# Filler matmuls, new gates for the weight loads, row-sum trips on another queue, and group sums by TensorE, in a fused attention and feed-forward kernel

## The chip, the cores and the metric

The kernel runs on one core of a Trainium2 chip. The metric is the device time of one execution in microseconds; before the change it was measured in three runs. The core's engines are TensorE (PE in the profile), VectorE (DVE), ScalarE (ACT), GpSimd (POOL) and SyncE (SP). Each works through its own instructions in order, and they meet through semaphores. DMA transfers are issued by an engine's queue (here SP's and POOL's).

## The reference

```python
def sm_attn(qq, kk, vv):
    s = scale * np.matmul(qq, kk.transpose(0, 1, 3, 2))
    s = s - np.max(s, axis=-1, keepdims=True)
    a = np.exp(s)
    a = a / (np.sum(a, axis=-1, keepdims=True) + 1e-09)
    return np.matmul(a, vv)
q_d = q.reshape(B, H, Sd, factor, D).mean(axis=3)      # factor 4; k_d, v_d likewise
out_up = np.repeat(sm_attn(q_d, k_d, v_d), factor, axis=2)
mask = np.abs(pos[:, None] - pos[None, :]) < factor
...                                                    # masked softmax attention: out_local
attn_out = out_up + out_local
x = attn_out.transpose(0, 2, 1, 3).reshape(B * S, H * D)
h = x @ w_in
out = (h * (1.0 / (1.0 + np.exp(-h))) @ w_out).astype(np.float32)
```

The inputs q, k and v have the shape (8, 8, 576, 64), float32; w_in is (512, 2048), w_out (2048, 512), and the output (4608, 512).

## The kernel before

The 64 heads are worked in 32 pairs; four pairs make a batch of 576 tokens by 512 features, which is what the feed-forward part takes. For each pair, SP loads q and k (names `qk`), the value rows in four pieces (`vs`), and from pair 8 on the values once more in groups of four rows (`vq`, three issues). Pairs 1 to 3 come as bf16 straight from POOL's queue (`SW`). POOL casts to bf16 (`qkb`, `vb`). TensorE transposes (`pe_T`, L785 for the transposes), VectorE and ScalarE copy the results out of PSUM (`qT`, `kT`), and the sums over groups of four rows (`qd`, `kd`) are made in one of two ways: for pairs below `GS_PE` = 8 by TensorE inside `pe_T`, with a selection matrix `idp`, and copied out (`group`); for later ones by two VectorE reductions (`reduce`, L830). Then come scores (`pe_S`), exponentials on ScalarE (`Pt` local, `Pd` grouped), row sums (`pe_Z`), reciprocals on VectorE (`zr`, L947), and the weighted values (`pe_PV1`, `pe_PV2`).

The reciprocals must be spread over partitions. Pairs below 8 do it by TensorE (`RB`). Later ones make a trip through DRAM: `z{p}` writes `zr` to `scr`, then two DMAs `b{p}0` and `b{p}1` read it back, each half broadcast to 64 partitions of `Rb`; all three are issued by SP (`Z_ENG`), in `after_Z`. VectorE multiplies (`xo`, L999) and POOL adds the two parts into `xT` (L1026), the feed-forward input.

The feed-forward part has nine super-blocks of 512 tokens. `g1` is the hidden layer, 16 units of four 128x512 matmuls each, followed by tanh on ScalarE (`th`, L1052) and a product on VectorE (`gT`, L1056); `g2` is the output layer, 16 units again, then a copy (`osb`) and a store from SP. G1 of super-block 0 needs pairs 0 to 3, of 1 pairs 0 to 7, of 2 pairs 0 to 11. All of w_in and w_out come in eight chunks from POOL's queue (`weights`, `w0` to `w7`; `w0` to `w3` are w_in, 1 MB each); the first unit of G2 needs `w4` to `w7`.

The order on every engine is written by a planner before the program is built. A job has engines, a planned cost, jobs before it (`pre`), buffers and PSUM banks that it takes, and a due time; `Plan.run` steps through time, gives each engine the ready job with the least due time (on TensorE, `pick` chooses between attention work, `A` and `V` jobs, and G1 and G2 units), and the emitted instructions run in that order on the chip, with the semaphores that the data need. TensorE's planned costs are multiplied by `COLD[1]` before `COLD[0]` us. Planned DMA transfers share one flow. From pair 8 on a visit (`V{n}`) joins the scores of pair n, the transposes of n + 1, the row sums of n - 1 and the weighted values of n - 2, and comes when 8 (n - 10) units of G1 and G2 are done, or when nothing else can run.

Two settings gate loads. `W_GATE` says after which jobs a weight chunk may be issued: `w0` and `w1` after none, `w2` after the cast `cq5`, `w3` after `cq6`, the others after `cq7`. `load_order` gives the loads' order on SP and their gates: pair 1 waits for the cast `ck1`, pairs 4 to 7 for the issue of pair 3's last v piece, pairs 8 and 9 until chunk `w5` has landed, pairs 10 and 11 until `w6` has. A gate on a landed transfer is a semaphore wait on the issuing queue, and everything behind it in that queue waits too.

Of the kernel before, what the change touches and what calls it, by code (L numbers as in the profile page):

```python
# [19 lines left out]
COLD = (26.0, 1.5)  # L20
N_QK, N_VS, N_VQ, N_QKB, N_VB, N_VD, N_T, N_P, N_ZR, N_RB, N_XO = 3, 4, 2, 5, 5, 5, 3, 4, 2, 4, 2
GS_PE = 8
# [12 lines left out]
Z_ENG = "SP"  # L35
CV_ENG = ("POOL", "ACT")
# [4 lines left out]
def G2_BANKS(j):  # L41
    return ((5,), (4,), (2,), (3,)) if j >= 7 else ((4,), (5,))
# [44 lines left out]
W_GATE = {0: (), 1: (), 2: ("cq5",), 3: ("cq6",), **{c: ("cq7",) for c in range(4, 8)}}  # L87
# [6 lines left out]
def load_order():  # L94
    o = ["kx", ("qk", 0), ("qk", 1), ("qk", 2), ("qk", 3), ("v", 0), ("v", 1), ("v", 2), ("v", 3)]
    for p in range(4, NPAIR):
        o += [("qk", p), ("v", p)] + ([("vq", p)] if p >= VP_PE else [])
    return o, {1: ["ck1"], **{p: ["lv311!"] for p in range(4, 8)}, **{p: ["w6"] for p in range(10, 12)}, 8: ["w5"], 9: ["w5"]}
# [129 lines left out]
class Job:  # L228
    __slots__ = ("name", "eng", "cost", "emit", "pre", "take", "use", "due", "work", "port", "kind", "bank", "marks",
                 "idx", "n", "succ", "start", "end", "ran", "last", "thr")  # L230

    def __init__(self, name, eng, cost, emit, **kw):
# [4 lines left out]
        self.due, self.work, self.port, self.kind, self.thr = 0.0, 0.0, False, None, None  # L237
        for k, v in kw.items():
            setattr(self, k, v)
        self.ran, self.last, self.succ, self.end = None, None, [], None  # L240


class Plan:
# [5 lines left out]
    def __init__(self):  # L249
        self.jobs, self.pools, self.bind = {}, {}, {}  # L250
        self.banks = [None] * 8
        self.seq = []
# [56 lines left out]
    def run(self, pick):  # L309
# [37 lines left out]
        def release(k):  # L347
# [3 lines left out]
            if k[0] == "bank":  # L351
                for b in self.bind[k]:
                    self.banks[b] = None
# [15 lines left out]
        def flow(now):  # L369
            live = [q for q in queues.values() if q]  # L370
            dt, t = now - fluid[0], fluid[0]
            while live and dt > 1e-9:
                step = min(min(q[0][1] for q in live) * len(live), dt)
                for q in live:
                    q[0][1] -= step / len(live)
# [10 lines left out]
            if live:  # L386
                v = fluid[1]
                at(now + min(q[0][1] for q in live) * len(live) + 1e-6, lambda v=v: v == fluid[1] and flow(clock[0]))
# [8 lines left out]
        def dispatch(e, now):  # L397
# [12 lines left out]
            for x in j.eng:  # L410
                ready[x].remove(j)
            self.grab(j)
# [45 lines left out]
def bass_hourglass_attn__then__act_silu_kernel(  # L458
# [9 lines left out]
    with kctx:  # L468
# [21 lines left out]
        osb = sb("osb", [128, 512], F32, 2)  # L490

# [155 lines left out]
        def dma(name, eng, out_, in_, r, w, sem, work, cost, hold=(), **kw):  # L647
            def emit(j):
                P.op(eng, lambda s: s.dma_start(out_(), in_()), r() if r else [], w(), sem(), after=gates(hold))  # L649
# [3 lines left out]
        def loads(p, order):  # L653
            if p == 0:
                dma("lkx", "SP", lambda: kx[64:128, :], lambda: rows(k, 0, 64, 0), None, lambda: rkx, lambda: "kx",
                    0.45, 0.43, due=order["kx"], take=[("qkb", -1)])
            for x, (t, n, off) in enumerate(((q, 128, 0), (k, 128 if p < NPAIR - 1 else 64, 64))):
                if p in SW:
                    dma(f"c{'qk'[x]}{p}", "POOL", lambda x=x, n=n: qkb[S("qkb", p)][0:n, x, :],
                        lambda t=t, n=n, off=off: rows(t, p, n, off), None, lambda x=x: [R(f"qkb{S('qkb', p)}{x}")],  # L660
                        lambda x=x: f"qkb{S('qkb', p)}{x}", 0.9, 0.9, take=[("qkb", p)], due=-60 + p)
                    continue
                dma(f"l{'qk'[x]}{p}", "SP", lambda x=x, n=n: qk[S("qk", p)][0:n, x, :],
# [3 lines left out]
            for h in range(2):  # L667
                for j in range(2):
                    def emit(jb, h=h, j=j):
# [5 lines left out]
                        if (p, h, j) == (0, 0, 0):  # L675
                            lo = 1
                            P.op("SP", lambda e: e.dma_start(vs[s][3:64, 0, :], bass.AP(
                                tensor=T_, offset=base.offset, ap=[[64, 61], [1, 64]])), [], w, sem, after=gates(["vz"] + list(order.get(("gate", p), ()))))
                        if (p, h, j) == (NPAIR - 1, 1, 1):
                            hi = 4  # L680
                            P.op("SP", lambda e: e.dma_start(vs[s][64:123, 9, :], bass.AP(
                                tensor=T_, offset=base.offset + 517 * D_, ap=[[64, 59], [1, 64]])), [], w, sem)
                        P.op("SP", lambda e: e.dma_start(d[:, lo:hi, :], bass.AP(  # L683
                            tensor=T_, offset=o + 58 * 64 * lo, ap=[[64, 64], [58 * 64, hi - lo], [1, 64]])), [], w, sem,
                            after=gates(order.get(("gate", p), ())))
                    J(f"lv{p}{h}{j}", "SP", 0.61, emit, work=0.39, take=[("vs", p)],
                      due=order["v", p], pre=list(order.get(("gate", p), ())) + (["vz"] if p == 0 else []))
            if p >= VP_PE:
# [10 lines left out]
                J(f"lvq{p}", "SP", 1.4, emit, work=1.0, take=[("vq", p)], due=order["vq", p],  # L699
                  pre=list(order.get(("gate", p), ())) + [f"vqz{(p - VP_PE) % N_VQ}"])  # L700

        def weights(c, due, pre):
# [10 lines left out]
            J(f"w{c}", "POOL", 0.9, emit, work=3.2, due=due, pre=pre)  # L713
# [230 lines left out]
        def after_Z(p, key, i, col_):  # L944
# [9 lines left out]
            J(f"r{p}", "DVE", 1.15 if p < RB_PE else 0.6, emit, pre=[f"Z{p}"] + (["ga", "gb"] if p < RB_PE else []),  # L954
              bank=[(key, ())], take=[("zr", p)], due=D(p, 4.0))
            if p < RB_PE:
                return
            dma(f"z{p}", Z_ENG, lambda: scr[S("Rb", p)][:, :], lambda: zr[S("zr", p)][:, :],
                lambda: [R(f"zr{S('zr', p)}")], lambda: [R(f"scr{S('Rb', p)}")], lambda: f"scr{S('Rb', p)}", 0.25, 0.43,
                pre=[f"r{p}"], use=[("zr", p)], take=[("Rb", p)], due=-1000 + p, kind="hot")  # L960
            for h in range(2):
                dma(f"b{p}{h}", Z_ENG, lambda h=h: Rb[S("Rb", p)][half(h), :],
                    lambda h=h: bass.AP(tensor=scr[S("Rb", p)].tensor, offset=scr[S("Rb", p)].offset + 64 * h * 72,
                                        ap=[[0, 64], [1, 720]]),
                    lambda: [R(f"scr{S('Rb', p)}")], lambda h=h: [R(f"Rb{S('Rb', p)}{h}")],
                    lambda h=h: f"Rb{S('Rb', p)}{h}", 0.6, 0.43, pre=[f"z{p}"], use=[("Rb", p)], due=-1000 + p, kind="hot")
# [10 lines left out]
        def RB(p, wants):  # L977
# [3 lines left out]
            def emite(jb):  # L981
# [3 lines left out]
                     [R(f"Rb{n}0"), R(f"Rb{n}1")])  # L985
            J(f"RB{p}", "PE", 0.4, emit, pre=[f"r{p}", "rsel2"], use=[("zr", p)], bank=[(("r", p), wants)], due=D(p, 2.8), kind="A")
            J(f"b{p}0", ("ACT", "DVE"), {"ACT": 0.8, "DVE": 0.85}, emite, pre=[f"RB{p}"], bank=[(("r", p), ())], take=[("Rb", p)],
              due=D(p, 2.4), marks={f"b{p}1": 1.0})
# [4 lines left out]
        def after_PV(p):  # L993
# [3 lines left out]
            def emitm(jb):  # L997
# [3 lines left out]
                    [rB[bb[0]], rB[bb[1]], R(f"Rb{u}0"), R(f"Rb{u}1")], [R(f"xo{x}")])  # L1001
# [26 lines left out]
            J(f"m{p}", "DVE", 0.92, emitm, pre=[f"PV{p}", f"b{p}0", f"b{p}1"], bank=[(("o", p), ())], use=[("Rb", p)],  # L1028
# [9 lines left out]
        def g1(j, f):  # L1038
# [24 lines left out]
            J(f"t{j}_{f}", "ACT", 0.61, emitt, pre=[f"g1_{j}_{f}"], bank=[(key, ())], take=[("th", n)], due=-2000 + n)  # L1063
            J(f"s{j}_{f}", "DVE", 0.70, emits, bank=[(key, ())], use=[("th", n)], due=-2000 + n,
# [222 lines left out]
```

## Time and profile before

| what | value |
|---|---|
| median of three runs | 406.34 us (404.93, 406.34, 406.6) |
| the profiled execution | 403.24 us, span 401.4 us |
| TensorE busy | 346.7 us (86% of the span) |
| VectorE, ScalarE, GpSimd busy | 226.2, 170.2, 155.0 us |
| mean granted clock of TensorE | 0.960 |
| G1 matmuls (576) | 176.6 us, 435 ns each |
| G2 matmuls (576) | 143.1 us, 387 ns each |

The span runs from the first to the last instruction. Matmuls overlap in the pipeline, so the mean of one is longer than its share of the time. "SPq" is SP's queue: time in which it issues a DMA or waits to. "issue" is time in which an engine waited for nothing that the profile shows. The granted clock is 1.00 at full speed; where the profile holds no record, at the start, it reads 1.00 as well.

### The profile page before, as it was taken

The numbers are of one execution on the slowest core, as the hardware profiler recorded it, in microseconds if no ns is written. First come the engines' busy times: TensorE is split into PE (matmuls) and PEld (weight loads), VectorE is DVE, ScalarE is ACT, GpSimd is POOL, SyncE is SP. The second block draws the span as 40 slices with busy tenths as digits, with TensorE's granted clock in tenths as the row PEclk, the third lists the DMA queues.
The fourth block names the chain that finished last, engine by engine and source line by source line (L and its number), as shares of the span: only waits on it lengthen the run. The fifth ranks groups of instructions, "written<-read, shape, count | busy, mean of one in ns | idle before, by whom it ended". The sixth has DMA issues, their size and how long they took to land.

```text
span 401.4 us, 12104 instructions
## 1 busy us (share of the span) xinstructions
PE 346.7 (86%) x5288; PEld 217.0 (54%) x5288; DVE 226.2 (56%) x395; ACT 170.2 (42%) x303; POOL 155.0 (39%) x177
## 2 busy tenths in 40 slices
PE   1557878989968598787997989999999999999996
PEld 1445656655634254545654546666656655566542
DVE  7246365767554455755656658877768534353300
ACT  3334356555433223443454444455555343444311
POOL 6014805395467556544643846564211210000000
PEclk9999599999996889996999999999999999999999
DMA  8975728987777878878897776442221310101022
GB/s 168 296 191 142 211 86 134 264 229 194 207 223 225 236 212 229 246 205 246 224 258 217 194 209 176 123 123 81 71 83 59 105 52 26 39 16 52 28 78 78
DMA packets 77823, 62.59 MB, mean 156 GB/s; under 512 B 50122, under 2 KB 60618, under 8 KB 77770
## 3 DMA queue, kind: packets, MB, share of 16 engines
q1 hardware_dynamic: 72682, 54.65, 48.4%
q0 software_dynamic: 5088, 7.18, 8.1%
q8 instruction: 41, 0.67, 0.7%
q14 instruction: 12, 0.10, 0.1%
HBM read 54.46 MB, written 10.32 MB: 161 GB/s over the span
## 4 chain that ended last, share of the span: by engine, by line
PE 64%; SPq 10%; DMA 8%; DVE 7%; issue 6%; POOL 2%; ACT 2%; POOLq 0%; DVEq 0%; ACTq 0%
PE PS L535 61%; DMA Rb<-scr 7%; SPq L683 4%; SPq L649 3%; PE PS L785 2%; SPq L696 2%; DVE gT L1056 2%; DVE xo L999 2%; DMA scr<-zr 1%; DVE qT L529 1%; ACT th L1052 1%; SPq L693 1%; POOL vt L758 1%; DVE zr L951 1%; POOL xT L1026 1%
## 5 line engine op out<-in xcount | busy, mean ns | idle before, releaser
L535 PE MATMUL PS<-xT,w_in_sb 128*128 128x512 f32 x576 | 176.6, 435 | 11.9 <-DVE gT L1056 11.6
L535 PE MATMUL PS<-w_out_bf,gT 128*128 128x512 bf16 x576 | 143.1, 387 | 4.4 <-DVE gT L1056 3.6
L1052 ACT ACTIVATE th<-PS 128x512 f32<-128x512 f32 x144 | 86.1, 598 | 134.9 <-PE PS L535 134.8
L535 PEld LDWEIGHTS PS<-xT,w_in_sb 128*128 128x128 f32 x576 | 107.3, 193 | 46.4 <-DVE gT L1056 18.7
L1056 DVE SCALAR_TENSOR_TENSOR gT<-th,PS 128x512 bf16<-128x512 f32 x144 | 97.5, 679 | 60.8 <-ACT th L1052 60.8
L535 PEld LDWEIGHTS PS<-w_out_bf,gT 128*128 128x128 bf16 x576 | 49.8, 99 | 76.7 <-issue 22.3
L1026 POOL TENSOR_TENSOR xT<-xo 128x576 fp32r<-128x576 f32 (+3 forms) x48 | 42.3, 895 | 84.6 <-DVE xo L999 84.6
L999 DVE TENSOR_TENSOR xo<-PS,Rb 128x720 f32<-128x720 f32 x32 | 28.9, 904 | 40.2 <-DMA Rb<-scr 33.3
L529 POOL CAST vb<-vs 128x640 bf16<-128x640 f32 x31 | 22.4, 722 | 60.8 <-PE PS L535 40.2
L1084 ACT ACTIVATE osb<-PS 128x512 f32<-128x512 f32 x36 | 21.6, 599 | 54.3 <-PE PS L535 54.3
L745 POOL CAST qkb<-qk 128x1152 bf16<-128x1152 f32 x28 | 33.6, 1199 | 10.5 <-DMA qk<-in_k_dram 10.5
L529 DVE COPY qT<-PS 128x576 bf16<-128x576 bf16 x30 | 22.7, 757 | 25.8 <-PE PS L785 18.0
L758 POOL TENSOR_TENSOR vt<-vq 128x512 f32<-128x512 f32 x24 | 31.6, 1315 | 9.3 <-DMA vq<-in_v_dram 8.7
L785 PE MATMUL PS<-idn,qkb 64*64 64x64 bf16 x1152 | 17.1, 205 | 11.1 <-DVE qkb L529 7.5
L947 DVE RECIPROCAL zr<-PS 128x72 f32<-128x72 f32 x32 | 19.2, 601 | 11.0 <-PE PS L535 11.0
L875 ACT ACTIVATE Pt<-PS 128x576 bf16<-128x576 f32 x32 | 20.7, 647 | 9.8 <-PE PS L535 9.8
L785 PEld LDWEIGHTS PS<-idn,qkb 64*64 64x64 bf16 x1152 | 14.0, 118 | 13.4 <-DVE qkb L529 7.5
L529 ACT ACTIVATE kT<-PS 128x576 bf16<-128x576 bf16 x29 | 19.3, 665 | 0.0
L763 POOL TENSOR_TENSOR vd<-vt 128x256 bf16<-128x256 f32 x24 | 17.7, 736 | 0.8
L830 DVE TENSOR_REDUCE qd<-qT 128x144 bf16<-128x576 bf16 x24 | 17.8, 742 | 0.0
L830 DVE TENSOR_REDUCE kd<-kT 128x144 bf16<-128x576 bf16 x24 | 17.8, 742 | 0.0
L881 DVE TENSOR_TENSOR Pt<-Pt,mask 128x576 bf16<-128x576 bf16 x24 | 17.6, 735 | 0.0
(67 smaller groups left out, 226.5 us busy)
## 6 DMA issues: line engine op xcount, KB each, us to landing
vs<-in_v_dram SPq DMA_DIRECT2D x126, 80.0 KB, 3.7
out_dram<-osb SPq DMA_DIRECT2D x36, 256.0 KB, 2.2
Rb<-scr SPq DMA_DIRECT2D x48, 180.0 KB, 3.6
qk<-in_q_dram SPq DMA_DIRECT2D x29, 288.0 KB, 3.5
qk<-in_k_dram SPq DMA_DIRECT2D x28, 288.0 KB, 5.5
vq<-in_v_dram SPq DMA_DIRECT2D x24, 256.0 KB, 4.1
w_in_sb<-in_moe_w_in_dram POOLq DMA_DIRECT2D x4, 1024.0 KB, 8.5
w_out_bf<-in_moe_w_out_dram POOLq DMA_DIRECT2D x4, 512.0 KB, 9.7
```

The lines of the kernel that those rows point to most:

```text
L529: return e.activation(out_, in_, AF.Copy) if eng == "ACT" else e.tensor_copy(out_, in_)
L535: P.op("PE", lambda t: t.matmul(out_, lhsT, rhs, start=start, stop=stop, skip_group_check=True), r, w)
L745: P.op("POOL", lambda e, a=i(), b=j(): e.tensor_copy(qkb[b][:, :, :], qk[a][:, :, :]), [R(f"qk{i()}0"), R(f"qk{i()}1")], [R(f"qkb{j()}0"), ...
L758: P.op("POOL", lambda g: g.tensor_tensor(vt[:, :, :], vq[n][:, :, 0:128], vq[n][:, :, 128:256], ALU.add), [R(f"vqm{n}"), R(f"vqe{n}0"), R( ...
L785: P.op("PE", lambda e, o=o, w=w, j=j: e.transpose(o, w, idn[half(j), :]), [R("idn"), R(f"qkb{n}{x}")], [rB[t]])
L830: P.op("DVE", lambda e: e.tensor_reduce(dst, src.rearrange("p (g r) -> p g r", r=4), AX.X, ALU.add), [R(f"{'qk'[x]}T{s}")], [R(f"{'qk'[x]} ...
L875: P.op("ACT", lambda e: e.activation(d[:, :, :], PS[:, b[0]:b[1] + 1, a:e_], AF.Exp, scale=sc), [rB[b[0]], rB[b[1]]], [R(f"P{m}" if local ...
L999: P.op("DVE", lambda e: e.tensor_tensor(xo[x][:, :, :], PS[:, bb[0]:bb[1] + 1, 0:360], Rb[u][:, :].rearrange("p (x c) -> p x c", x=2), ALU ...
L1026: P.op("POOL", lambda g, dst=dst, in0=in0, in1=in1: g.tensor_tensor(dst, in0, in1, ALU.add), [R(f"xo{x}")], xblk(kc, t + a, t + e_))
L1052: P.op("ACT", lambda e: e.activation(th[x][:, :], PS[:, b, :], AF.Tanh, scale=0.5), [rB[b]], [R(f"th{x}")])
L1056: P.op("DVE", lambda e: e.scalar_tensor_tensor(gT[j % 2][:, f, :], th[x][:, :], 1.0, PS[:, b, :], ALU.add, ALU.mult), [rB[b], R(f"th{x}")] ...
L1084: P.op("ACT", lambda e, s=S("osb", n), b=bank(key)[0]: e.activation(osb[s][:, :], PS[:, b, :], AF.Copy, scale=0.5), [rB[bank(key)[0]]], [R ...
```

## The change

- **Filler matmuls.** A tile `dz` (128x512, bf16, all ones) is set at the start. Where the planner sees TensorE idle and a PSUM bank free, up to `WARM_END` = 115 planned us, matmuls of `dz` with itself (128x512) are put ahead of the next TensorE job: before 7 us as many of 0.43 us as fit into the idle time less 0.4 us, later as many of 0.22 us as fit into 0.6 of it. Their results are not read.
- **Gates.** `w0` to `w3` wait until the last v piece of pairs 2, 5, 6 and 7 has landed, `w4` to `w7` until the vq loads of pairs 8 to 11 have. Loads of pair 8 wait for `w2` in place of `w5`; the gates of pairs 9 to 11 go.
- **Row-sum trips.** `z` and `b` are issued by ScalarE's queue, and the two `b` become one DMA of 128 partitions.
- **Group sums.** `GS_PE` goes from 8 to 12.
- **Planner.** Planned costs of many jobs change, mostly up for TensorE; transfers share the flow by a weight of their packets (`gran`); the cold factor is 1.65 until 8 us. For super-blocks 0 to 6 G2 may take banks 6 and 7 too. The v casts of pairs 0 to 3 are POOL's alone. `S_DUE` and `LD_ENG` are new names for the values that stood there.

```diff
-COLD = (26.0, 1.5)
+COLD = (8.0, 1.65)
+WARM_END, WARM_GAP, WARM_PART = 115.0, 0.4, 0.6
-GS_PE = 8
+GS_PE = 12
-Z_ENG = "SP"
-CV_ENG = ("POOL", "ACT")
+def Z_ENG(p):
+    return "ACT"
+CV_ENG = "POOL"
 def G2_BANKS(j):
-    return ((5,), (4,), (2,), (3,)) if j >= 7 else ((4,), (5,))
+    return ((5,), (4,), (2,), (3,)) if j >= 7 else ((4,), (5,), (6,), (7,))
-W_GATE = {0: (), 1: (), 2: ("cq5",), 3: ("cq6",), **{c: ("cq7",) for c in range(4, 8)}}
+W_GATE = {0: ("lv211",), 1: ("lv511",), 2: ("lv611",), 3: ("lv711",), 4: ("lvq8",), 5: ("lvq9",), 6: ("lvq10",), 7: ("lvq11",)}
-    return o, {1: ["ck1"], **{p: ["lv311!"] for p in range(4, 8)}, **{p: ["w6"] for p in range(10, 12)}, 8: ["w5"], 9: ["w5"]}
+    return o, {1: ["ck1"], **{p: ["lv311!"] for p in range(4, 8)}, 8: ["w2"]}
...
+            if e == "PE":
+                b = min((b for b in range(8) if self.banks[b] is None), key=lambda b: self.freed[b], default=None)
+                if b is not None:
+                    j.idle = (now - max(busy["PE"], self.freed[b]), b)
...
+        dz = sb("dz", [128, 512], BF16)
...
-            for h in range(2):
-                dma(f"b{p}{h}", Z_ENG, lambda h=h: Rb[S("Rb", p)][half(h), :],
-                    lambda h=h: bass.AP(tensor=scr[S("Rb", p)].tensor, offset=scr[S("Rb", p)].offset + 64 * h * 72,
-                                        ap=[[0, 64], [1, 720]]),
+            dma(f"b{p}0", Z_ENG(p), lambda: Rb[S("Rb", p)][:, :],
+                lambda: bass.AP(tensor=scr[S("Rb", p)].tensor, offset=scr[S("Rb", p)].offset,
+                                ap=[[64 * 72, 2], [0, 64], [1, 720]]),
...
-            J(f"T{p}", "PE", 0.65 if p < GS_PE else 0.33, lambda jb: pe_T(p), kind="A", due=D(p, 8.5), **tk(p))
+            J(f"T{p}", "PE", 0.85 if p < GS_PE else 0.4, lambda jb: pe_T(p), kind="A", due=D(p, 8.5), **tk(p))
...
+        J("dz", "DVE", 0.15, lambda jb: P.op("DVE", lambda e: e.memset(dz[:, :], 1.0), [], [R("dz")]), due=-300)
...
+            if jb.ran == "PE" and jb.idle is not None and jb.start < WARM_END:
+                room = jb.idle[0] - WARM_GAP if jb.start < 7.0 else (jb.idle[0] - WARM_GAP) * WARM_PART
+                cost = 0.43 if jb.start < 7.0 else 0.22
+                for _ in range(int(room / cost)):
+                    mm(PS[:, jb.idle[1], :], dz[:, 0:128], dz[:, :], [R("dz")], [rB[jb.idle[1]]], True, True)
             jb.emit(jb)
```

## The prediction

> **What bounds the kernel now.** I read the page first, then the windows cut at the kernel's stages, then the chain and the two lists of waits, and last the order of time on SP and TensorE.
>
> The first G1 matmuls (hidden layer) start at 43.8 us, pair 8's scores at 89.1, G1 of super-block 2 at 142 (it needs pairs 8 to 11), and SP's loads end at about 254. The windows cut there show each stage's limit:
>
> ```profile
> core 0: us, PE busy (x) PEld busy (x) DVE busy (x) ACT busy (x) POOL busy (x), PEclk, DMA share, GB/s
> 0.00:43.80 43.80, 21.66 (x925) 17.94 (x925) 23.17 (x85) 15.73 (x29) 15.56 (x26) 0.94 0.83 201
> 43.80:89.00 45.20, 39.91 (x800) 27.54 (x796) 27.77 (x47) 23.95 (x45) 23.40 (x26) 0.94 0.79 179
> 89.00:142.00 53.00, 43.75 (x807) 25.17 (x807) 29.59 (x47) 20.35 (x37) 31.83 (x40) 0.89 0.77 216
> 142.00:250.00 108.00, 93.72 (x1383) 58.26 (x1381) 68.50 (x104) 46.31 (x82) 58.12 (x61) 0.96 0.79 222
> 250.00:300.00 50.00, 49.38 (x720) 30.87 (x718) 38.28 (x58) 24.91 (x44) 21.16 (x24) 1.00 0.32 95
> ```
>
> From 250 on TensorE is full at clock 1.00. Before that it idles 22.1, 5.3, 9.3 and 14.3 us, and its clock is halved in part of each stage. Nobody else is full by this table. The chain names the missing resource, SP's queue:
>
> ```profile
> PE 64%; SPq 10%; DMA 8%; DVE 7%; issue 6%; POOL 2%; ACT 2%; POOLq 0%; DVEq 0%; ACTq 0%
> ```
>
> Of the chain between 84 and 145 us alone, SP's issues are 23% and "DMA Rb<-scr", the row-sum trip's last leg, 19%. SP's own waits and those of the others say why:
>
> ```profile
> SPq L649 <- DMA w_out_bf<-in_moe_w_out_dram: 28.5, 1, 28.5
> SPq L649 <- DVE zr L947: 22.9, 8, 4.2
> SPq L649 <- DMA scr<-zr: 11.4, 9, 2.6
> ```
> ```profile
> DVE xo L999 <- DMA Rb<-scr: 33.3, 14, 5.7
> POOL vb L529 <- DMA vs<-in_v_dram: 20.7, 7, 14.2
> PE PS L535 <- issue: 12.4, 7, 4.3
> ```
>
> Two faults. First, SP stands still 28.5 us, until chunk w5 has landed; in order of time:
>
> ```profile
> 39.45 2.60 SPq L683 DMA_DIRECT2D vs<-in_v_dram  x4
> 70.52 0.33 SPq L649 DMA_DIRECT2D qk<-in_q_dram  x1
> ```
>
> So pairs 8 and later come late. All 32 G1 units of super-blocks 0 and 1 (93 of their 128 matmuls by 89 us) are done by 111, and none runs until 142. Second, from there SP is never idle: between 110 and 250 us its waits sum to about 11 of 140 us, and a visit takes 9.7 us (scores of pair 8 at 89.1, of pair 26 at 263.4: 174.3/18).
>
> At the start the page's "issue" waits matter:
>
> ```profile
> 16.68 0.26 PE L535 MATMUL PS<-qd,kd 64*64 64x72 bf16 x1 [4.26 <-issue]
> 22.88 0.25 PE L535 MATMUL PS<-qT,kT 64*64 64x56 bf16 x2 [3.01 <-issue]
> ```
>
> They fall inside a group that needs nothing new, 128 matmuls apart (1+9+36+60+4+18), while DMA runs at a share of 1.24. The instruction queue moved 41 packets, 0.67 MB, which is 256 instructions of 64 B each (estimated): TensorE waits for its program behind the 2 MB of w0 and w1.
>
> **The change, part by part.** The sum is against the profiled execution, 403.24 us (span 401.4 and 1.84 around it); the median, 406.34, is 0.8% more.
>
> *Weight gates and load gates.* Leaves the start: w0 and w1, 1 MB each, now behind pair 2's and pair 5's v. At the 297 GB/s of 10 to 20 us, 2 MB are 7 us. The first v cast, at 21.0 after 14.2 us of waiting, and the program's fetches come up to that much earlier. Bounds for the first G1: 0 (the chain goes on through DVE and ScalarE) and 10 us (all issue waits before 43.8). I take 5, nearer the chain's mixed rows. Pair 8's gate is now w2, behind pair 6's last v. That v is issued by 30.6 and lands 3.7 later; w2 takes 8.5: 43 us, or 36 to 43 after the start's gain, against 70.5. Pair 8 then waits for pair 7 (scores at 65.8, some 5 to 8 earlier with the start), so its scores come near 62 to 64 instead of 89.1: 25 us. Bounds: 8 (only the start's shift) and 30. Everything up to super-block 2's G1 moves with it. TensorE's account allows it: from 36 to 117 us it has 81 us; pairs 4 to 7 take about 3.3 each and visits 8 to 11 1.4 each (104.76 to 106.17), 19 us; 60 units of four matmuls at 0.896 take 54 (after 300 us the windows by tile hold 181 + 240 matmuls, 105 units, in 98.2 busy us with three visits: 94/105); 8 are left for stalls. That is the 60 units that before had done by 142. Term: **-25**.
>
> G2 needs w4 to w7, now behind the vq loads of pairs 8 to 11. These move up with the visits; w7 lands at some 77 to 80 (four issues of 0.76, landing 9.7). G1's 32 units cover until 36 + 29 + 19 = 84. With that cover gone, each us late is one of idle TensorE. POOL's queue now holds at eight landings; behind it stand casts and the xT adds. POOL is idle 50 of the first 89 us, so I take 0; the bound is eight times 3.7 us.
>
> *Row-sum trips to ScalarE.* SP loses 24 z issues (0.43) and 48 b issues (0.60): 1.6 us a pair, and the waits on zr and scr, 34 us in all. What is left is q, k, v, vq and outputs: 0.86 + 2.5 + 1.5 + 0.6 = 5.5 us a pair. That is under TensorE's 8 x 0.896 + 1.4 = 8.6 a visit, so TensorE should lead again between 142 and 250, where it loses 14.3 us idle and about 5 to half clock. I take 15 of 19 back; bounds 0 and 19. Term: **-15**. The price is on ScalarE's queue: z 0.43 and one b of 0.6 (as one half now) to 1.2 (two halves), 1.0 to 1.6 a pair. Behind them stand tanh, then DVE's gT, then a PSUM bank. ScalarE has 119 us idle from 89 to 300, which hides 25 to 39. A wait is not hidden: z's landing was 2.4 us in the median and 3.9 between 110 and 240, and the planner holds about 2.4 free. 0 to 1.5 a pair, 0 to 36 in all; ScalarE idles more than half the time, so I put a tenth on TensorE: **+3**. POOL takes a v cast over (0.72), hidden likewise.
>
> The Trainium skill's first page ("Trainium Kernel Development and Optimization", Key Constraints) says that all queues share the same 16 DMA engines and that issuing from several engines saves only issue time. By it the trip's 4.1 us landing stays, DVE's wait for Rb with it, and this term would be some 5 instead of 15. The trace has no second hardware queue to decide it.
>
> *Constant matmuls.* TensorE idles 28 us before 115 us. If the plan has as much, some 15 run before the first transposes (0.43 each, to about 7.3 us; those start at 7.47) and 50 later. Gain: 43.8 to 48.9 ran at clock 0.5, worth 2.5, and the first four pairs' groups shrink (a transpose group 1.5 to 0.96 us, V selection 1.07 to 0.69), 8 us in all, perhaps 3 on the chain. These are in the 25 above (5 + 3 = 8 at the start). Price: 0 if all fall into waiting, 50 x 0.22 = 11 if none does. Waits rule these stages, so **+1**. Two instructions each are half a fetch of 256.
>
> "TensorE: Matmul & The Clock Gate" (Why this matters) asks only that idle gaps stay under about 3 us. The profile speaks against it as the whole rule: before the clock fell at 38.6 us, the gaps were 0.74, 0.20 and 1.23 us. By the page the fillers would gain nothing there and the start's 8 be 5.
>
> *Group sums by TensorE, pairs 8 to 11.* Off DVE: eight reductions of 0.742; on: eight short copies (0.3). On TensorE 0.45 each: **+1.8**, and two more fetches, hidden. *Planner costs and banks* move order only: taken as 0, bounds -5 and +5 (the idle of 43.8 to 89).
>
> Sum: 403.24 - 25 - 15 + 3 + 1 + 1.8 = 369. On the median's scale **372**.
>
> **Rivals.**
> 1. *Early start only* (0.20). The cadence stays at 9.7 us, since Rb's landing of 4.1 us or POOL's casts take SP's place. For: DVE's 33.3 us of waiting for Rb. Against: POOL is busy 5.4 of 10 us, and the DMA share of 0.79 has been 1.24. 403.2 - 25 + 6 = 384, on the median's scale 387.
> 2. *TensorE full throughout* (0.10). First G1 at 36, work 258 + 13 + 34, 5 added, 3 at the end: 349; with what lies around it and scaled, 353.
> 3. *ScalarE becomes the bound* (0.10), slower. Each visit holds its queue for the whole trip. The end is 64 + 23 visits x c + 93.6 (pair 31's scores to the end before). It equals 401.4 at c = 10.6. ScalarE's work is 4.2 a visit plus 1.6, so holds of 4.8 us decide: z's 3.9 plus 0.95 of DVE wait is just there. With gT's 0.7 on top, c = 11.3 and the time is 419. Against: the planner places b after its own 2.4 us.
> 4. *No change* (0.02): gains and holds cancel.
>
> **How the numbers follow.** Forecast 0.58, rivals as given. The range runs from rival 2's 353 to 392: rival 1's 387 and some us of z holds. Left out: half of rival 2, rival 3, a tail of rival 1. Measurements of this kernel tell 0.5% (404.93 to 406.6). Faster 0.88, same 0.02, slower 0.10. In the forecast alone the range is 358 to 384.
>
> **What would show it.** Right: first G1 at 34 to 39 us; SP's wait for a weight under 5 us; pair 8's scores at 60 to 68; G1 of super-block 2 at 110 to 120; clock 1.00 from 10 to 115; visits under 9 us; DVE's wait for Rb under 12 us. Wrong: ScalarE waiting long for scr or zr; TensorE idle before the first G2; matmuls of dz on the chain; POOL held by v landings while casts wait.

## The result and the profile after

The changed kernel takes **516.2 us** (median of 512.36, 516.07, 516.33 and 517.7), against 405.63 us before (403.78 to 406.6): a ratio of 1.272, with a 95% interval of 1.263 to 1.280. The forecast was 372 us with a range of 353 to 392. The kernel became 110 us slower where 34 us of gain were forecast, and none of the rivals reached that far; the slowest of them ended at 419. The ratios in this document leave disturbed runs out and the medians are over all runs of a kernel, so that the two need not divide out exactly.

The profiled execution of the changed kernel has a span of 515.9 us and a mean granted clock of 0.858 (before: 401.4 us and 0.960). Its chain, by engine, is no longer led by TensorE:

```profile
DMA 52%; PE 35%; DVE 8%; issue 4%; ACT 1%; DVEq 0%; ACTq 0%
```

SP's queue, 10% of the chain before, has left it, as forecast. But DMA went from 8% to 52%: the breakdown by line gives 41.5% to `Rb<-scr`, the read-back of the row-sum trip, and 10.7% to `scr<-zr`, the write ahead of it. The list of waits (engine, line, releaser: us in total, times, longest) has the same name near its top, and what hangs on it:

```profile
DVE xo L1020 <- DMA Rb<-scr: 132.0, 24, 12.3
...
PE PS L557 <- DVE gT L1077: 64.9, 19, 6.2
...
ACT th L1073 <- DVE zr L969: 50.2, 8, 8.3
...
PE PS L557 <- DVE xo L1020: 30.1, 6, 10.8
PE PS L557 <- issue: 20.2, 21, 3.3
...
ACT th L1073 <- DMA scr<-zr: 12.8, 4, 4.2
```

VectorE waits for `Rb` at every one of the 24 trips, 5.5 us each, where before it waited 14 times and 33.3 us in all. The other rows follow from it: VectorE works in order, so `zr` and `gT` stand behind the held `xo`; ScalarE and TensorE stand behind those. The chain in order of time (start, length, what) shows three visits of the late part, one trip after the other:

```profile
342.28 2.36 DMA scr<-zr
344.64 0.02 issue
344.66 10.35 DMA Rb<-scr
355.01 0.02 issue
355.04 0.91 DVE xo L1020
...
358.30 10.73 DMA Rb<-scr
369.02 0.02 issue
369.05 0.91 DVE xo L1020
369.95 0.53 DVE zr L969
370.48 0.02 issue
370.50 1.50 DMA scr<-zr
372.00 0.02 issue
372.02 9.89 DMA Rb<-scr
```

A visit is now a read-back of some 10 us and little else. The windows of the changed kernel (stretch, length, then busy time and count of PE, PEld, DVE, ACT and POOL, clock, DMA share, GB/s) say what the rest of the chip does meanwhile:

```profile
140.00:250.00 110.00, 71.33 (x912) 42.46 (x919) 41.96 (x64) 27.63 (x50) 43.85 (x46) 0.76 0.62 167
250.00:300.00 50.00, 38.60 (x534) 23.59 (x538) 23.62 (x36) 16.41 (x30) 17.65 (x20) 0.83 0.45 135
300.00:398.00 98.00, 74.42 (x1054) 45.43 (x1064) 51.74 (x81) 34.88 (x63) 30.29 (x35) 0.93 0.24 74
```

Between 250 and 300 us TensorE was full before, at clock 1.00; now it idles a quarter of the time in all three stretches and more in the first, and the clock is down in part of each. The DMA share tells most: between 300 and 398 us the DMA engines are used to 24%, and the read-back still takes 10 us. So there is little other traffic that it could wait for.

From one visit to the next (`xo` of pair 8 to `xo` of pair 26, by 18) it takes 14.1 us, where before it took 9.7. From pair 8's `xo` to pair 31's it is 310.1 us instead of 209.8, and these 100 us are most of the 110 that the kernel lost.

SP, finally, is what the forecast wanted it to be, relieved:

```profile
SPq L671 <- ACT osb L1105: 249.8, 35, 21.6
...
SPq L671 <- DMA w_in_sb<-in_moe_w_in_dram: 7.5, 1, 7.5
```

It waits 249.8 us for outputs to store, and the wait for a weight chunk fell from 28.5 to 7.5 us. By itself that bought nothing.

### The profile page after: what moved, and what is told of

Its sections match the earlier page's. It is cut to its first block, busy times and chain, and to the rows that moved or that the text cites. A ratio compares the mean times of both kernels' runs of the same rounds, so it can differ in the third digit from the quotient of the medians.

```text
span 515.9 us, 12557 instructions
## 1 busy us (share of the span) xinstructions
PE 386.2 (75%) x5521; PEld 239.6 (46%) x5556; DVE 224.8 (44%) x387; ACT 170.2 (33%) x307; POOL 155.8 (30%) x182
## 4 chain that ended last, share of the span: by engine, by line
DMA 52%; PE 35%; DVE 8%; issue 4%; ACT 1%; DVEq 0%; ACTq 0%
DMA Rb<-scr 41%; PE PS L557 34%; DMA scr<-zr 11%; DVE xo L1020 3%; DVE zr L969 1%; DVE gT L1077 1%; PE PS L807 1%; DVE zr L973 0%; ACT kT L551 0%; DVE qT L551 0%; DVE mbias L592 0%; ACT th L1073 0%; DVE vsel L592 0%; DVE cv L592 0%; DVE qd L852 0%
## 5 line engine op out<-in xcount | busy, mean ns | idle before, releaser
L557 PE MATMUL PS<-xT,w_in_sb 128*128 128x512 f32 x576 | 193.7, 471 | 65.9 <-DVE gT L1077 64.9
L557 PEld LDWEIGHTS PS<-xT,w_in_sb 128*128 128x128 f32 x576 | 119.5, 215 | 108.7 <-DVE gT L1077 75.6
L557 PE MATMUL PS<-w_out_bf,gT 128*128 128x512 bf16 x546 | 146.4, 409 | 3.7 <-issue 2.4
L557 PEld LDWEIGHTS PS<-w_out_bf,gT 128*128 128x128 bf16 x576 | 52.5, 104 | 79.3 <-issue 33.5
L1105 ACT ACTIVATE osb<-PS 128x512 f32<-128x512 f32 x36 | 21.5, 597 | 57.5 <-PE PS L557 41.5
L557 PE MATMUL PS<-Pt,vb 64*64 64x58 bf16 (+1 forms) x640 | 12.8, 209 | 29.6 <-DVE xo L1020 29.6
L767 POOL CAST qkb<-qk 128x1152 bf16<-128x1152 f32 x28 | 32.5, 1165 | 1.4 <-DMA qk<-in_k_dram 1.4
L557 PEld LDWEIGHTS PS<-Pt,vb 64*64 64x64 bf16 x640 | 9.7, 123 | 32.4 <-DVE xo L1020 30.8
L897 ACT ACTIVATE Pd<-PS 128x432 bf16<-128x432 f32 x32 | 17.1, 533 | 10.4 <-DMA scr<-zr 10.4
L557 PEld LDWEIGHTS PS<-qT,kT 64*64 64x64 bf16 x640 | 9.8, 117 | 15.6 <-issue 14.6
```

The costliest lines, as they stand in the source:

```text
L557: P.op("PE", lambda t: t.matmul(out_, lhsT, rhs, start=start, stop=stop, skip_group_check=True), r, w)
L767: P.op("POOL", lambda e, a=i(), b=j(): e.tensor_copy(qkb[b][:, :, :], qk[a][:, :, :]), [R(f"qk{i()}0"), R(f"qk{i()}1")], [R(f"qkb{j()}0"), ...
L897: P.op("ACT", lambda e: e.activation(d[:, :, :], PS[:, b[0]:b[1] + 1, a:e_], AF.Exp, scale=sc), [rB[b[0]], rB[b[1]]], [R(f"P{m}" if local ...
L1105: P.op("ACT", lambda e, s=S("osb", n), b=bank(key)[0]: e.activation(osb[s][:, :], PS[:, b, :], AF.Copy, scale=0.5), [rB[bank(key)[0]]], [R ...
```

## The experiments

Five sets, each on one chip beside the kernel before: e asks about the read-back, f takes parts of the change back, g and h try parts alone (g4 goes with f), and i changes the order alone. That kernel's medians were 401.98, 404.21, 404.46, 405.08 and 404.82 us.

### The read-back as one DMA

The theory: the merged `b` is slow because of its shape. Its source is `[[64*72, 2], [0, 64], [1, 720]]`, with an outermost dimension of 2. The rival: ScalarE's queue holds it (rival 3 of the forecast).

**e1_halves_act** is the changed kernel with the read-back issued as two halves, in the same job on ScalarE's queue, so that the order on all engines stays what it is:

```diff
-            dma(f"b{p}0", Z_ENG(p), lambda: Rb[S("Rb", p)][:, :],
...
-                                ap=[[64 * 72, 2], [0, 64], [1, 720]]),
...
+                for h in range(2):
+                    P.op(j.ran, lambda s, h=h: s.dma_start(Rb[S("Rb", p)][half(h), :], bass.AP(
+                        tensor=scr[S("Rb", p)].tensor, offset=scr[S("Rb", p)].offset + 64 * h * 72, ap=[[0, 64], [1, 720]])),
```

> The changed kernel with the one read-back of the row sums issued as two DMAs of 64 partitions, as before the change, still on ScalarE's queue and inside the same planner job, so the order on every engine is unchanged. Theory S (the slowest dimension of the merged read has size 2, so two DMA engines carry its 360 KB): Rb lands in 3 to 5 us instead of 10 to 16, visits take 8.5 to 9.5 us, 370 to 400 us in all. Rival Q (ScalarE's queue itself is slow to issue or to land): Rb stays at 9 us or more, 480 to 515 us. Rival P (the plan, its gates and banks hold the visits, the trip is only where the wait shows): 480 to 515 us, with another wait in Rb's place.

**e2_merged_sp** is the changed kernel with `z` and the merged `b` on SP:

```diff
 def Z_ENG(p):
-    return "ACT"
+    return "SP"
```

> The changed kernel with z and the merged b issued by SP instead of ScalarE. Theory S: Rb still takes 9 us or more, 460 to 540 us. Rival Q: Rb lands in about 4 us, 375 to 405 us. Rival P: about 500 us with Rb landing in about 4.

**e3_halves_k4** is e1 with each half's source split so that its outermost dimension is 4:

```diff
-... offset=scr[S("Rb", p)].offset + 64 * h * 72, ap=[[0, 64], [1, 720]])),
+... offset=scr[S("Rb", p)].offset + 64 * h * 72, ap=[[0, 4], [0, 16], [1, 720]])),
```

> The changed kernel with two read-backs of 64 partitions whose source has a slowest dimension of 4 (4 x 16 broadcast rows in place of 64), same bytes and order. Theory S: four engines carry each 180 KB, so each half takes about as long as a merged read with half its bytes per engine and both overlap: 5 to 11 us, 410 to 500 us, between the run with plain halves and the changed kernel. If a broadcast is slow for its repeated reads and not for its slowest dimension, it equals the run with plain halves. Rival Q and rival P: as the changed kernel, 500 to 520 us.

**e4_before_merged** is the kernel before with the merged `b` on SP, in the place of the first half; the second half's job issues nothing:

```diff
-            for h in range(2):
-                dma(f"b{p}{h}", ... ap=[[0, 64], [1, 720]] ...)
+            dma(f"b{p}0", ... ap=[[64 * 72, 2], [0, 64], [1, 720]] ...)
+            J(f"b{p}1", Z_ENG, 0.6, lambda j: None, ...)
```

> The kernel before with one edit: the two read-backs of a pair become the merged one, on SP, the second planner job issuing nothing. Theory S: Rb takes 9 us or more and each visit that waits for it lengthens by 3 to 6 us: 450 to 520 us. Rivals Q and P: 400 to 410 us, since neither ScalarE's queue nor the new plan is in it.

Measured, with the median time from the end of the last `b` issue to the start of `xo` over the 24 trips:

| kernel | outermost dimension | median us | ratio (95%) | issue to `xo`, us | visit, us |
|---|---|---|---|---|---|
| before | 64, two halves | 401.98 | 1 | 4.1 | 9.7 |
| e1_halves_act | 64, two halves | 414.22 | 1.027 (1.017, 1.036) | 5.0 | 9.2 |
| e3_halves_k4 | 4, two halves | 457.97 | 1.139 (1.128, 1.149) | 6.7 | 11.2 |
| e4_before_merged | 2, one DMA, SP | 502.82 | 1.250 (1.239, 1.262) | 10.0 | 13.4 |
| e2_merged_sp | 2, one DMA, SP | 511.75 | 1.272 (1.261, 1.284) | 9.8 | 13.3 |
| the change | 2, one DMA, ScalarE | 516.2 | 1.272 (1.263, 1.280) | 11.2 | 14.1 |

The time goes with the shape and not with the queue. Merging costs 101 us in the kernel before (401.98 to 502.82) and 98 to 102 in the changed one (414.22 to 511.75 with the trip on SP, on one chip; to 516.2 on another). From ScalarE to SP the ratio stays at 1.272. With 4 in the outermost place it stands between, though e1 and e3 issue the same two DMAs of the same bytes to the same partitions; so it is not the number of DMAs either. The rival is out. e1 itself was expected at 370 to 400 us and took 414: what else the change holds costs some 12 us, and the next set goes after them. VectorE's wait for `Rb` says the same in e1, e2, e3 and e4, in this order:

```profile
DVE xo L1021 <- DMA Rb<-scr: 31.9, 15, 4.1
```
```profile
DVE xo L1020 <- DMA Rb<-scr: 122.8, 24, 9.6
```
```profile
DVE xo L1021 <- DMA Rb<-scr: 78.7, 22, 8.8
```
```profile
DVE xo L999 <- DMA Rb<-scr: 123.0, 24, 8.8
```

The DMA queues, asked for one read-back, show how (packets, MB, share of 16 engines). In the changed kernel, 404.3 to 413.8 us, after the issue of a `b` at 403.74, with no load or store beside it and only a `z` of 36 KB behind it:

```profile
q10 hardware_dynamic: 274, 0.41, 12.6%
```

A share of 12.6% of 16 engines is the work of 2.0 engines, busy through the whole 9.5 us at 21 GB/s each. In e3, 354.6 to 358.0 us, this queue's share is 3.7 engines (an output store ran beside it, on another queue):

```profile
q10 hardware_dynamic: 78, 0.21, 23.0%
```

And in e1, 295.8 to 297.8 us, 7.7 engines in the mean over the 2 us in which the same 0.37 MB pass:

```profile
q10 hardware_dynamic: 160, 0.37, 48.3%
```

From the two medians of the change and e3 one can work out a fixed part and a share of work: 11.2 = 2.2 + 18/2 and 6.7 = 2.2 + 18/4. With 16 engines that would be 3.3 us; 4.1 to 5.0 were measured, beside other traffic. This is an estimate: two numbers give two medians exactly, and the merged read-backs on SP, at 9.8 and 10.0, would give less.

The Trainium skill has the rule on its page "DMA: Bandwidth & Descriptors". The section "Why a DMA increments its semaphore by 16 and not by 1" says that a DMA uses the largest number of engines up to 16 that divides the slowest dimension, other than 1, of both of its access patterns; "Rules for kernel authors" adds that an outermost dimension below 16, such as "a leading zero-stride broadcast of c copies", confines it to at most c engines. For 2, 4 and 64 this gives 2, 4 and 16 engines; the shares above agree for 2 and 4, and for 64 they exceed 4 without showing all 16.

### The parts of the change, taken back one by one

These start from e1, with the read-back in halves; e1 was still 2.7% slower than before.

**f1_gates_before**: e1 with `W_GATE` and the gates of `load_order` as before.

```diff
-W_GATE = {0: ("lv211",), 1: ("lv511",), 2: ("lv611",), 3: ("lv711",), 4: ("lvq8",), ...}
+W_GATE = {0: (), 1: (), 2: ("cq5",), 3: ("cq6",), **{c: ("cq7",) for c in range(4, 8)}}
-    return o, {1: ["ck1"], ..., 8: ["w2"]}
+    return o, {1: ["ck1"], ..., **{p: ["w6"] for p in range(10, 12)}, 8: ["w5"], 9: ["w5"]}
```

> From here on the base is the changed kernel with its read-back in two halves (414 us, where before takes 402 on the same chip). This run gives it back the weight gates and load gates of before. Theory G (the gates: the four w_out chunks are issued at 69 to 91 us, among the loads of pairs 8 to 11, so G2 starts at 116 instead of 91 us and G1 of super-block 2 no earlier than before): 392 to 404 us, first G2 copy at about 95. Rival A (the trip on ScalarE's queue costs the 12 us): 410 to 418 us. Rival F (the fillers cost it): 410 to 418.

**f2_trip_sp**: e1 with `z` and the halves on SP.

```diff
 def Z_ENG(p):
-    return "ACT"
+    return "SP"
```

> The base of two halves with z and both halves issued by SP again. Theory G: 410 to 418 us. Rival A: 396 to 406 us, and ScalarE's waits for zr, scr and unseen causes (the osb copy's 14 us, tanh's 15) gone. If the move helps, as predicted for SP's saturated queue, it is slower: 418 to 430.

**f3_no_fillers**: e1 without one `dz` matmul.

```diff
-                for _ in range(int(room / cost)):
+                for _ in range(0):
                     mm(PS[:, jb.idle[1], :], dz[:, 0:128], dz[:, :], [R("dz")], ...)
```

> The base of two halves without one filler matmul (20 to 23 of them were issued). Theory G and rival A: within 3 us of the base, 411 to 417 us, a cold clock from the first matmul on. Rival F: 400 to 408 us. If the fillers help: 417 to 422.

**f4_before_gates**: the kernel before with the new gates alone.

```diff
-W_GATE = {0: (), 1: (), 2: ("cq5",), ...}
+W_GATE = {0: ("lv211",), 1: ("lv511",), 2: ("lv611",), 3: ("lv711",), 4: ("lvq8",), ...}
```

> The kernel before with the new weight and load gates alone. Theory G: 408 to 418 us, G2 later than 91 us. Prediction's step (early pair 8, minus 25 us): 375 to 385. Rivals A and F: 398 to 404, as before.

**g4_f1_trip_sp**: f1 with the same edit, the trip on SP.

> The best version so far (two halves, the gates of before, 402.3 us against 404.2) with the trip on SP again. What is left of the change is the planner's costs, the fillers and the group sums. If ScalarE's queue helps by 1%: 404 to 408 us. If it holds tanh as rival A says: 395 to 401. Theory T: 400 to 404, no difference.

| kernel | median us | ratio (95%) |
|---|---|---|
| f1_gates_before | 402.25 | 0.990 (0.983, 0.996) |
| f2_trip_sp | 403.9 | 0.997 (0.994, 1.001) |
| f3_no_fillers | 409.19 | 1.016 (1.010, 1.021) |
| f4_before_gates | 402.23 | 0.997 (0.993, 1.001) |
| g4_f1_trip_sp | 407.14 | 1.005 (1.001, 1.009) |

Either of two parts taken back returns the 2.7%: the gates (f1, 0.990) or ScalarE's queue (f2, 0.997). So theory G, which puts the loss on the gates alone, holds for f1 and fails for f2 and f4.

The new gates, priced at 25 us of gain, do nothing alone (f4, 0.997). They do what they say on SP. In f4 its wait for a chunk is

```profile
SPq L649 <- DMA w_in_sb<-in_moe_w_in_dram: 12.7, 1, 12.7
```

instead of 28.5 us, and SP issues pair 8's q, in the changed kernel's order of time, not at 70.5 us but here:

```profile
33.23 2.60 SPq L705 DMA_DIRECT2D vs<-in_v_dram  x4
52.15 0.33 SPq L671 DMA_DIRECT2D qk<-in_q_dram  x1
```

That is 18 us earlier. But pair 8's scores came at 84.0 us in the changed kernel, at 82.5 in e1 and at 85.2 in f4, against 89.1 before: 4 to 7 us earlier, where 25 were forecast. In TensorE's order they stand behind the attention chain of pairs 4 to 7 and the G1 units that the planner put among them. Pair 7's scores did not move (66.2 us in e1, 65.8 before), and its part of the feed-forward input was complete at 82.9 us in the changed kernel and 81.4 in e1, against 79.6 before. So the loads of pair 8 were early, and TensorE was not ready for them.

The same gates also put w_out later. POOL issued all four chunks at 60.9 to 63.9 us before. In the changed kernel, in order of time, the first and the last are

```profile
69.03 0.78 POOL L734 DMA_DIRECT2D w_out_bf<-in_moe_w_out_dram  x1
...
92.08 0.78 POOL L734 DMA_DIRECT2D w_out_bf<-in_moe_w_out_dram  x1
```

and the first output copy (`osb`), the end of a first group of G2, starts at 123.8 us instead of 95.5 (f4: 112.5).

### The parts alone, on the kernel before

**g1_before_trip_act**: the kernel before with `z` and both halves of `b` on ScalarE's queue.

```diff
-Z_ENG = "SP"
+Z_ENG = "ACT"
```

> The kernel before with z and both halves of b issued by ScalarE, nothing else. The prediction's step (SP's queue sets the 9.7 us of a visit, minus 15): 385 to 393 us, visits at 8.6 to 9.0 us. Theory T (TensorE with its own small stalls sets the visit, SP was busy but not late): 398 to 406 us, visits at 9.3 to 9.8 us, SP now waiting for the output copies instead of issuing.

**g2_before_no_trip**: the planned order of before, where `z` and `b` of pairs 8 to 31 issue nothing. It leaves out the spreading of these pairs' row sums, so it is only a bound.

```diff
-            dma(f"z{p}", Z_ENG, ...)
+            J(f"z{p}", Z_ENG, 0.25, lambda j: None, work=0.43, ...)
-                dma(f"b{p}{h}", Z_ENG, ...)
+                J(f"b{p}{h}", Z_ENG, 0.6, lambda j: None, work=0.43, ...)
```

> The kernel before in the same planned order, with neither z nor b issued for pairs 8 to 31: each such pair multiplies by what its Rb buffer holds from a pair below 8, so the row sums of 24 pairs are left out. This bounds what any change of the trip can win. The prediction's step: 380 to 390 us. Theory T: 393 to 402 us; DVE's 33 us of waiting for Rb were mostly time in which TensorE had units to run.

**g3_before_fillers**: the kernel before with the filler matmuls, by the rule of the change.

```diff
+            if jb.ran == "PE" and jb.idle is not None and jb.start < WARM_END:
...
+                for _ in range(int(room / cost)):
+                    mm(PS[:, jb.idle[1], :], dz[:, 0:128], dz[:, :], ...)
```

> The kernel before with the filler matmuls alone, 27 of them. Prediction's step (clock kept, minus 3 to 5 us at the start and between 44 and 49): 396 to 400 us. Rival (fillers too few and too far apart to hold the clock, and each a little in the way): 401 to 407 us, the clock halved from about 14 us on as in the changed kernel.

**h1_trip_gates**: g1 with the new gates, the edit of f4.

> The kernel before with the trip on ScalarE in two halves (394.9 us, the base of this set), and the new weight and load gates. If the gates and ScalarE's queue disturb each other (chunks of w_out among the loads delay z, and ScalarE holds tanh for it): 403 to 415. If the early loads help once SP is free, as the prediction has it: 375 to 390. If gates are neutral: 392 to 398.

**h2_trip_gs12**: g1 with the group sums of pairs 8 to 11 on TensorE.

```diff
-GS_PE = 8
+GS_PE = 12
```

> The same base and the group sums by TensorE for 12 pairs. Prediction's step: plus 1.8 us on TensorE, 395 to 398. If DVE's queue was in the way of the trip (kd waits 7.0 us of TensorE): 388 to 393. If the extra matmuls wait for their program: 399 to 405.

**h3_trip_fillers**: g1 with the fillers, the edit of g3.

> The same base and the fillers (27). Neutral, as on the kernel before: 393 to 399. If they are what spends the 20 us: 403 to 412.

**h4_trip_costs**: the changed kernel with the read-back in halves, the gates of before, no fillers and `GS_PE = 8`. Against g1 it keeps the planner's new costs, flow weights and cold factor, the two further G2 banks, and the v casts on POOL alone.

```diff
-GS_PE = 12
+GS_PE = 8
-W_GATE = {0: ("lv211",), ...}
+W_GATE = {0: (), 1: (), 2: ("cq5",), ...}
-                for _ in range(int(room / cost)):
+                for _ in range(0):
```

> The changed kernel with halves, the gates of before, no fillers and group sums for 8 pairs: what is left beside the trip is the planner's new costs, flow weights, cold factor, G2's banks 6 and 7 and the v casts. If the costs alone spend the gain: 400 to 408. If they are neutral, as the prediction took them: 392 to 398.

| kernel | median us | ratio (95%) |
|---|---|---|
| g1_before_trip_act | 394.87 | 0.972 (0.960, 0.983) |
| g2_before_no_trip | 374.38 | 0.925 (0.918, 0.933) |
| g3_before_fillers | 406.48 | 0.998 (0.992, 1.004) |
| h1_trip_gates | 401.84 | 1.001 (0.994, 1.009) |
| h2_trip_gs12 | 407.74 | 1.007 (0.999, 1.015) |
| h3_trip_fillers | 397.44 | 0.984 (0.976, 0.992) |
| h4_trip_costs | 416.13 | 1.026 (1.017, 1.035) |

h2 and h4 lie above all that was expected of them. **g1 is the best version found**: 394.87 us, 10 less than before. It is what the forecast's second term described, without the rest. Its waits on ScalarE, VectorE and TensorE, and the same stretch of the windows as above, in the kernel before and in g1:

```profile
ACT osb L1084 <- DMA scr<-zr: 18.5, 3, 7.7
...
DVE xo L999 <- DMA Rb<-scr: 7.9, 7, 2.1
...
PE PS L785 <- ACT osb L1084: 7.0, 4, 2.3
```
```profile
140.00:250.00 110.00, 95.65 (x1426) 59.55 (x1426) 69.85 (x107) 46.31 (x82) 60.03 (x64) 0.95 0.79 221
```
```profile
140.00:250.00 110.00, 103.50 (x1533) 63.85 (x1532) 79.72 (x118) 50.51 (x91) 62.99 (x69) 0.97 0.83 216
```

Of 110 us TensorE is busy 103.5 instead of 95.65. VectorE's wait for `Rb` went from 33.3 to 7.9 us (and 7.5 us ahead of `xo` without a releaser in the profile, 4.4 before), although the landing itself did not shorten (4.7 us from issue to `xo`, 4.1 before): the trip starts sooner, because it no longer stands in SP's queue behind loads. From the end of `zr` to the issue of the first `b` it takes 3.7 us in the mean, 5.4 before. A visit takes 9.2 us. The price is there as well: ScalarE is held by a landing of `z` three times, 18.5 us in all, and TensorE's wait for ScalarE's `osb` went from 1.1 to 7.0 us. g2 bounds what any trip could give in this order: with none, 374.38 us, 30 less than before and below both of its expectations.

Nothing else of the change adds to g1. Fillers 2.6 us, gates 7, group sums 13 and the planner's new costs 21 us are lost on top of it, by medians taken on different chips; how much of this is the order alone is asked next.

### How much the order alone moves

Each of these parts also gives the planner other inputs, and it writes another order. The last two runs change the inputs by next to nothing.

**i1_before_reordered** is the kernel before, and **i2_trip_reordered** is g1, with 0.02 us on two planned costs of the pairs below 9:

```diff
-            J(f"Z{p}", "PE", 0.27, ...
+            J(f"Z{p}", "PE", 0.29, ...
-            J(f"PV{p}", "PE", 0.32, ...
+            J(f"PV{p}", "PE", 0.34, ...
```

> The kernel before with the planned costs of Z and PV for pairs below 9 raised by 0.02 us each (0.27 to 0.29, 0.32 to 0.34); no instruction added or removed, the order of TensorE's work differs from the first G1 on. If the order alone moves the time by some per cent: outside 400 to 408 us, either way. If not: 401 to 407.

> The same two costs in the kernel with the trip on ScalarE in halves (394.9 us). If the order alone moves the time: outside 391 to 399, most likely above, 399 to 410, since that order was a good draw. If not: 392 to 398, and the parts that took the gain back did it by what they do.

Measured: i1 406.22 us, ratio 1.007 (1.002, 1.011), and i2 403.24 us, 0.987 (0.979, 0.995). The instructions are the same, and their order on TensorE differs from the first G1 unit on; the time moves by 0.7% and, against g1's 0.972, by 1.6%, though the intervals of g1 and i2 overlap. So a part of this size can't be told from its reordering, and g1's 10 us may be in part a lucky order: reordered, the same kernel is at 0.987, some 5 us below the kernel before, or 2% below i1, which has the same two costs.

Put together, gates and queue make a small table (ratios to before):

| | trip on SP | trip on ScalarE |
|---|---|---|
| planner of before, gates of before | 1 | 0.972 (g1) |
| planner of before, new gates | 0.997 (f4) | 1.001 (h1) |
| changed planner with sums and fillers, gates of before | 1.005 (g4) | 0.990 (f1) |
| changed planner with sums and fillers, new gates | 0.997 (f2) | 1.027 (e1) |

Under both planners the trip on ScalarE gains with the old gates; with the new ones it gains nothing (h1) or loses (e1). Between the two sets of gates it differs by 3.3 and 4.5 points. That is more than reordering moved in i1 and i2, but two reorderings are no bound. The late w_out accompanies it (first `osb` at 93.9 us in g1, 121.4 in h1), but f4 has it late too and loses nothing. In the profiles the loss lies behind the visits: pair 31's `xo` starts at 302.6 us in h1 and 307.3 in g1, and 92.9 us follow it in h1, 85.3 in g1. **This interaction is open.** Open as well is why group sums and the planner's new costs lose 13 and 21 us on top of g1, while f1, which has both, ends at 0.990.

## Why the prediction was wrong

**The merged read-back, +100 us, is the step that failed.** "Row-sum trips to ScalarE" priced it as issue time, 0.6 to 1.2 us a pair, and carried the landing of 4.1 us over from the two halves. Nothing in the profile of before had that shape, so the landing had to be bounded from both sides, and it wasn't. It is 11.2 us. The visit grew from 9.7 to 14.1, and from pair 8's `xo` to pair 31's the kernel took 100 us longer. With the halves put back (e1) the same kernel and order take 414 us, so the merged read-back makes the kernel slow, and the rest of the change, 1.027, is no gain either. The skill's sentence that was weighed, that issuing from several engines saves only issue time, is about the queue; the rule that bore on it was the one on how many engines a DMA uses, and the diff showed the 2.

**Weight and load gates, -25.** Failed too. The load of pair 8 did come earlier, at 52.2 us where 36 to 43 were forecast: the 30.6 us of the sum is when pair 5's last v was issued, pair 6's was issued by 34.5, and w2 went out only at 45.7, in POOL's order behind an xT add and two casts. The step then put pair 8's scores right behind the load, "some 5 to 8 earlier with the start" for pair 7. With the gates alone the start gave nothing (first G1 at 44.9 in f4, 43.8 before), and with the rest of the change 0.8 to 2 us (43.0; 41.7 in e1); only f3, without fillers, has it 5 us earlier, at 38.9. The "issue" waits stayed: 11.5 us in f4 and 20.2 in the changed kernel, 12.4 before. In the changed kernel the first of them ends at 13.3 us, and POOL issues the first weight chunk at 17.8, so w0 and w1 are not what that wait was for; what it was for is not shown. And what stands ahead of pair 8 in TensorE's written order is not late loads but work. The cover for w_out failed too: "w7 lands at some 77 to 80" supposed vq loads that came with the visits; w7 was issued at 92.1.

**Trips to ScalarE, -15 + 3.** Right in mechanism, and of the right sign where it can be read: g1 gives -10 and its reordered twin i2, at 0.987, some -5, where -12 were forecast. ScalarE's holds were 18.5 us in g1, of which 6 show in TensorE's wait for `osb`. The visits became 9.2 us, not 8.6. SP stopped waiting for `zr` and `scr`, 34 us before, with its loads behind them, so more than issue time left it. With the 5 that the forecast took from the skill's sentence, the two terms would have made -2; g1 and i2 lie between -2 and -12, and the runs do not decide. With the new gates the gain is gone, which the sum of terms could not say.

**Constant matmuls, +1.** The size is not contradicted: the fillers cost nothing clear of noise in g3 (0.998), 2.6 us in h3 against g1 and 5.0 in e1 against f3, on different chips and in different orders. The count was wrong: the trace has 23, 19 of them by 115 us, where some 65 were expected; 13 stand ahead of the first transposes. TensorE in order of time:

```profile
1.46 5.73 PE L557 MATMUL PS<-dz 128*128 128x512 bf16 x13 [1.46 <-DVE vs L1211]
7.95 0.48 PE L807 MATMUL PS<-idn,qkb 64*64 64x64 bf16 x36 [0.76 <-DVE qkb L551]
...
13.28 0.24 PE L557 MATMUL PS<-qT,kT 64*64 64x58 bf16 x6 [2.31 <-issue]
...
17.56 0.31 PE L557 MATMUL PS<-qT,kT 64*64 64x58 bf16 x6 [2.44 <-issue]
```

When the first transposes run, their group has shrunk from 0.69 to 0.48 us (36 in both), and the profile's record of the clock begins with 1.00 at 7.4 us; in the kernel before it begins at 31.8. After a gap of 2.3 us, that ends at 13.3, the clock is halved from 14.2 us on, for 30.7 us (in e1 for 13.7); the next gap, of 2.4 us, lies in that stretch. These "issue" waits are not idle time that the planner sees, so no filler stands in them.

**Group sums, +1.8, and planner costs, 0 (±5).** Both too low where they could be read at all: +13 and +21 us on top of g1, of which the order may account for some 2 to 8 (the moves of i1 and i2).

**The rivals.** Rival 3 had the sign, so that the chance given to "slower" was right by luck and not by its cause: e2 takes ScalarE out of the trip and stays at 511.75. Rival 1 named the right resource, `Rb`'s landing, and left it at its old 4.1 us. Of the signs named ahead, "wrong" came as ScalarE waiting for `zr` (50.2 us), and that was an effect of VectorE being held.

## What to carry to other kernels

When two DMAs become one, compare the outermost dimensions of both access patterns before counting the issue saved: half a microsecond of issue a pair was bought with 6 to 7 us of landing, on a path with one trip a visit. No run here made the read-back one DMA with a wide outermost dimension, so what merging alone would do is not shown. A wait that vanishes from one queue is worth only what the next engine's written order lets through, so look for what stands ahead of the freed work there. And where a planner rewrites the order at each edit, measure its reordering by an edit of no size first, since several sound parts can sum to less than one of them.

## What the runs showed that was not expected

- A DMA that keeps two engines busy shows as a DMA share of 0.13 to 0.2 in the windows, with a transfer on the chain; a DMA system that looks idle and a kernel that waits for a DMA go together. Here it held from 340 us to the last trip, at 424.
- A small transfer behind such a read-back waits for it. In the changed kernel a `z` of 36 KB was issued at 405.71 us, 2 us behind a `b`, and landed 8.1 us later, as the `b` ended. Of the ten `z` after 300 us, the six that were issued while a `b` was under way took 2.4 to 8.1 us, and each landed within 1 us after the start of the `xo` that this `b` held; the other four took 1.5 to 2.0.
- 0.02 us on two planned costs moved the measured time by 0.7 and 1.6%, with the same instructions (the second of these between two chips).
